# New start addresses for the streamed tiles and the weights of an MLP, in a kernel of linear attention and MLP

## The chip, the cores and the metric

The kernel runs on one core of a Trainium2 chip. The metric is the device time of one execution in microseconds (us), taken as the median of several runs. A run of the profiler gives one execution in detail: which engine worked when, and on what.

The engines are TensorE (PE for its matmuls, PEld for the loads of its weights), VectorE (DVE), ScalarE (ACT), GpSimd (POOL) and SyncE (SP, which issues DMAs). They work on SBUF, a memory of 128 partitions in which a tile occupies the same byte addresses in each partition. An address below is the byte address within a partition, and "896 modulo 2048" is its remainder.

## The reference

An attention with a state that decays per channel feeds an MLP without biases, whose activation is ELU. All is float32; B, H, S, D are 4, 8, 768, 48, the model width is 384 and the hidden width 2048.

```python
def _attn_ref(r, k, v, w, u):
    for t in range(S):
        kt, vt, rt, wt = k[:, :, t], v[:, :, t], r[:, :, t], w[:, :, t]
        cur = einsum('bhd,bhe->bhde', u[None] * kt, vt)
        y[:, :, t] = einsum('bhd,bhde->bhe', rt, state + cur)
        state = wt[:, :, :, None] * state + einsum('bhd,bhe->bhde', kt, vt)

def _moe_ref(x, w_in, w_out):            # x: 3072 tokens x 384
    h = x @ w_in                         # 384 x 2048
    g = where(h > 0, h, exp(minimum(h, 0)) - 1)
    return g @ w_out                     # 2048 x 384
```

## The kernel before, in words

The sequence is cut into 6 chunks of 128 steps. A unit is one chunk of one batch entry, 24 in all. For each unit DVE turns the decays into running products (lines L387 and L397) and scales r and k by them. PE then computes scores (L458), transposes k (L466), forms the outer products for the state (L505) and the output of the attention (L488, tile pa_y), all in float32. Four units of a chunk together give the MLP's input for 512 tokens: 3 planes of 128 channels by 512 tokens.

The MLP works in float32r, a float32 that PE takes in one pass. To keep precision, each operand is split into a high part and the rest, and each product is made of three: high by high, high weights by the rest, and the rest of the weights by high. So there are weights w_h and w_l, inputs xh and xl, and hidden activations gh and gl. For one block f of 128 hidden units (16 blocks a chunk), the step g1 runs 3 planes x 3 products = 9 matmuls into the tile ph (L248): weights of 128 x 128 are loaded, and the 512 tokens of a plane of xh or xl stream through. ACT and DVE then compute ELU in the tile m (L253 and L256 on ACT, L259 on DVE), ACT writes gh (L266) and DVE gl (L270). The step g2 runs 9 matmuls from gh and gl into three accumulators acc (L281). In the first two chunks, blocks 0 to 5 are done in two halves of 256 tokens each, so that the MLP can start before all four units are ready; in the last block of the last chunk the last accumulator is done in two halves as well.

PE streams one operand of a matmul and holds the other as weights. In the MLP the streamed tiles are xh, xl, gh and gl, and each matmul has a load of 128 x 128 weights, a block of 512 bytes per partition, from w_h or w_l.

The weights arrive raw, in tiles wraw and wrawx, and are converted by ACT (L540, L549) and DVE (L545, L552) during the first chunks. wrawx is kept in the space of xh and xl of the odd chunks, which are not in use yet. x tiles are allocated in x_high (one pair for even chunks, one for odd), gh and gl in g_tile inside the function mlp (two buffers each), all from a pool of SBUF called home. A pool named pad, of PAD bytes, lies ahead of it and serves only to shift it. The weights lie in a pool called big at the start of memory.

The order of work on each engine is written out by hand in a table (ORDER), and tiles are handed on by rings of buffers (SLOTS); neither depends on addresses.

What runs ahead of the MLP in a warm-up are some matmuls of the tile ident (L367).

Of the kernel before, what the change touches and what calls it, by code (L numbers as in the profile page):

```python
# [8 lines left out]
F32 = mybir.dt.float32  # L9
F32R = mybir.dt.float32r  # L10
# [11 lines left out]
P = 128  # L22
# [5 lines left out]
NK = DM // P  # L28
N = B * C
# [23 lines left out]


COLS = 128
PAD = 576
FILL = {}
DIAG = ["PE"] * 8 + ["POOL"] * 16
SPREAD = ["ACT"] * 8 + ["POOL"] * 16
# [169 lines left out]
def mlp(nc, w_h, w_l, ps_acc, ps_h, ml, gp, po, dst, last=False):  # L229

    act, stt_ = nc.scalar.activation, nc.vector.scalar_tensor_tensor
    acc = []

    def accs():
        if not acc:
            acc.extend(ps_acc.tile([P, N], F32, tag=f"acc{m}", name=f"acc{m}") for m in range(NK))
        return acc

    def g1(s, x, fill=()):
        f, lo, hi = s["f"], s["lo"], s["hi"]  # L240
        xh, xl = (z[:, :, lo:hi] for z in x)
        s["ph"] = ph = ps_h.tile([P, N], F32, tag="ph", name="ph")[:, 0:hi - lo]
        for m in fill:
            nc.tensor.matmul(ph[:, 0:P], m, m, start=True, stop=True)
        for k in range(NK):
            for n, (w, x_) in enumerate(((w_h, xh), (w_h, xl), (w_l, xh))):
                for z in range(0, P, COLS):
                    nc.tensor.matmul(ph[z:z + COLS], w[:, f, 0, k, z:z + COLS], x_[:, k, :],  # L248
                                     start=(k == n == 0), stop=(k == NK - 1 and n == 2))

    def r1(s):
        s["m"] = ml.tile([P, N], F32, tag="m", name="m", bufs=2)[:, 0:s["hi"] - s["lo"]]
        act(s["m"], s["ph"], AF.Relu, scale=-1.0)  # L253

    def r2(s):
        act(s["m"], s["m"], AF.Exp, scale=-1.0)  # L256

    def stt(s):
        stt_(s["m"], s["m"], -1.0, s["ph"], ALU.add, ALU.max)  # L259

    def g_tile(n, s):
        return gp.tile([P, N], F32R, tag=n, name=n, bufs=2)[:, 0:s["hi"] - s["lo"]]

    def gh(s):
        s["gh"] = g_tile("gh", s)
        nc.scalar.copy(s["gh"], s["m"])  # L266

    def gl(s):
        s["gl"] = g_tile("gl", s)
        nc.vector.tensor_tensor(s["gl"], s["m"], s["gh"].bitcast(F32), ALU.subtract)  # L270

    def g2(s):
        f, lo, hi = s["f"], s["lo"], s["hi"]
        for m in range(NK):
            parts = 2 if (f == NF - 1 and m == NK - 1 and last) else 1
            for q in range(parts):
                s_ = slice(q * (hi - lo) // parts, (q + 1) * (hi - lo) // parts)
                a_ = accs()[m][:, lo + s_.start:lo + s_.stop]
                for n, (w, g) in enumerate(((w_h, s["gh"]), (w_h, s["gl"]), (w_l, s["gh"]))):
                    for z in range(0, P, COLS):  # L280
                        nc.tensor.matmul(a_[z:z + COLS], w[:, f, 1, m, z:z + COLS], g[:, s_],  # L281
                                         start=(f == n == 0 and lo == 0), stop=(f == NF - 1 and q == parts - 1 and n == 2))

    box = {}

    def out(m):
        if m == 0:
            box["o"] = po.tile([P, NK, N], F32, tag="wraw", name="o", bufs=1)
        o = box["o"]
        if not last:  # L290
            nc.scalar.copy(o[:, m], acc[m])
        elif m == 0:
            nc.scalar.copy(o[:, m], acc[m])
            send(m)
        elif m == 1:
            nc.vector.tensor_copy(o[:, m], acc[m])
        else:
            h = N // 2
            nc.scalar.copy(o[:, m, 0:h], acc[m][:, 0:h])
            send(1)  # L300
            nc.vector.tensor_copy(o[:, m, h:N], acc[m][:, h:N])
            send(m)

    def send(m):
        nc.scalar.dma_start(dst[m * P:(m + 1) * P], box["o"][:, m])

    def store(m):
        if not last:
            nc.sync.dma_start(dst[m * P:(m + 1) * P], box["o"][:, m])

    return dict(g1=g1, r1=r1, r2=r2, stt=stt, gh=gh, gl=gl, g2=g2, out=out, store=store, accs=accs)
# [3 lines left out]
def rwkv_elu_kernel(ctx, tc, wkr, rk, vp, u, uz, gkrw, gv, gu, w_in, w_out, out):  # L315
# [5 lines left out]
    big = keep("big", 1)  # L321
    kp = keep("kp", 1)
    pad, home = pool("pad", 1), pool("home", 1)
# [9 lines left out]
    flags = kp.tile([R2, NU], F32, name="flags")  # L333
    good = kp.tile([1, 1], I32, name="good")
    ones_c = kp.tile([R2, 1], F32, name="ones_c")
    w_h = big.tile([P, NF, 2, NK, P], F32R, name="w_h")
    w_l = big.tile([P, NF, 2, NK, P], F32R, name="w_l")
    pad.tile([P, PAD // 4], F32, name="pad")
    reset = cst.tile([R2, 2, NP, CW], F32, name="reset")
# [9 lines left out]
    raws, xts, pfs = {}, {}, []  # L349
# [140 lines left out]
    def x_high(u_):  # L490
        c, b = u_["c"], u_["b"]
        if c not in xts:
            xts[c] = [home.tile([P, NK, N], F32R, tag=n + str(c % 2), name=n, bufs=1) for n in ("xh", "xl")]
        nc.scalar.copy(xts[c][0][:, :, b * C:(b + 1) * C], u_["py"])

    def x_low(u_):
# [77 lines left out]
    for u_ in units:  # L574
        i, c, b = u_["i"], u_["c"], u_["b"]
# [37 lines left out]
        if b:  # L613
            after.append(("v", i - 1))
        add(("v", i), "PE", lambda u_=u_: value(u_), after)
        add(("xh", i), "ACT", lambda u_=u_: x_high(u_), [("v", i)])
        add(("xl", i), "DVE", lambda u_=u_: x_low(u_), [("xh", i)])
        if c < NC - 1:
# [10 lines left out]
    for c in range(NC):  # L629
        fns = mlp(nc, w_h, w_l, ps_acc, ps_h, ml, home, stg, out[:, c * N:(c + 1) * N], last=c == NC - 1)  # L630
        for f, lo, hi in steps[c]:
            s, n = dict(f=f, lo=lo, hi=hi), len(seq)
# [22 lines left out]
    for u_ in units:  # L655
        i, c = u_["i"], u_["c"]
# [156 lines left out]
```

## Time and profile before

| what | value |
|---|---|
| median of 3 runs | 520.03 us (518.87, 520.03, 521.28) |
| profiled execution: its own time | 521.82 us |
| profiled execution: its span, first to last instruction | 520.1 us |
| granted TensorE clock, mean | 0.995 |
| busy: PE, DVE, ACT, POOL | 502.2, 331.2, 276.1, 66.0 us |
| HBM read, written | 41.92 MB, 4.72 MB |

The page of a profile lists groups of instructions as: line, engine, operation, tile written <- tiles read, shape, count | busy us, mean ns of one | idle us before them and what ended it. L248 is line 248 of the kernel. For a matmul "ph<-xh,w_h" the tile xh is streamed and w_h is held as weights. Matmuls overlap in the pipeline, so the mean duration of one (some 390 ns at 512 columns) is longer than the time from one start to the next, which is what a stretch of matmuls costs. Windows are stretches of the span in us, with each engine's busy time and count in them.

### The profile page before, as it was taken

Reading aid. Unit: us, or ns where it says so; the run is one execution under the profiler, and the core shown is the slowest. Engines: PE = TensorE matmul, PEld = TensorE weight load, DVE = VectorE, ACT = ScalarE, POOL = GpSimd, SP = SyncE. Lnnn points to the kernel's source line nnn. Section 1 sums busy time; section 2 is a strip of 40 time slices with the busy share of each in tenths; the row PEclk is TensorE's granted clock in tenths of the full one; section 3 lists DMA queues with packets and bytes.
Section 4 is the critical chain, followed back from the end, with each engine's and each line's share of the span. In section 5 each row is a group of like instructions: output and inputs, shape, how many; then the busy total and the mean of one; then the engine's idle time right before and its main releaser. Section 6 shows DMA issues by size and latency. Waiting matters only on the chain.

```text
span 520.1 us, 10015 instructions
## 1 busy us (share of the span) xinstructions
PE 502.2 (97%) x4065; PEld 423.7 (81%) x4065; DVE 331.2 (64%) x533; ACT 276.1 (53%) x558; POOL 66.0 (13%) x74
## 2 busy tenths in 40 slices
PE   4999999999999999999999999999999999999994
PEld 4788988889988888788888888888888788878884
DVE  7998889967677765756757476647474744333332
ACT  4979798757554434635444445325744524544441
POOL 2000000002131130701203021020220210000000
PEclk9989999999999999999999999999999999999999
DMA  7969463322224231322121336001440100000001
GB/s 223 325 218 281 140 204 113 92 68 88 78 77 134 86 100 39 124 87 88 56 70 38 94 105 194 2 1 38 143 127 8 69 1 1 26 36 3 0 2 64
DMA packets 26596, 47.35 MB, mean 91 GB/s; under 512 B 2736, under 2 KB 9008, under 8 KB 26544
## 3 DMA queue, kind: packets, MB, share of 16 engines
q1 hardware_dynamic: 26112, 45.86, 28.6%
q8 instruction: 34, 0.56, 0.4%
q10 hardware_dynamic: 432, 0.79, 0.4%
q14 instruction: 18, 0.15, 0.1%
HBM read 41.92 MB, written 4.72 MB: 90 GB/s over the span
## 4 chain that ended last, share of the span: by engine, by line
PE 86%; DVE 5%; ACT 2%; issue 1%; DMA 1%; SPq 0%; DVEq 0%; ACTq 0%
PE ph L248 36%; PE acc L281 36%; PE pa_y L488 6%; PE pa_s L458 4%; PE pa_u L505 2%; PE pa_t L466 1%; DVE m L259 1%; DMA r<-in_wkr_dram 1%; PE pa_d L428 1%; DVE gl L270 1%; DVE am L461 1%; ACT gh L266 0%; DVE r L401 0%; ACT m L256 0%; DVE xl L498 0%
## 5 line engine op out<-in xcount | busy, mean ns | idle before, releaser
L248 PE MATMUL ph<-xh,w_h 128*128 128x512 f32 (+1 forms) x324 | 122.1, 377 | 1.1 <-DVE m L259 1.0
L253 ACT ACTIVATE m<-ph 128x512 f32<-128x512 f32 (+1 forms) x108 | 59.3, 549 | 118.6 <-PE ph L248 78.6
L281 PE MATMUL acc<-gh,w_h 128*128 128x512 f32 (+1 forms) x325 | 120.7, 371 | 0.0
L248 PE MATMUL ph<-xl,w_h 128*128 128x512 f32 (+1 forms) x324 | 119.4, 369 | 1.2 <-DVE xl L498 1.2
L259 DVE SCALAR_TENSOR_TENSOR m<-m,ph 128x512 f32<-128x512 f32 (+1 forms) x108 | 67.0, 624 | 82.5 <-ACT m L256 82.2
L248 PE MATMUL ph<-xh,w_l 128*128 128x512 f32 (+1 forms) x324 | 119.5, 369 | 0.0
L281 PE MATMUL acc<-gl,w_h 128*128 128x512 f32 (+1 forms) x325 | 119.0, 366 | 0.3 <-DVE gl L270 0.3
L281 PE MATMUL acc<-gh,w_l 128*128 128x512 f32 (+1 forms) x325 | 118.7, 365 | 0.0
L270 DVE TENSOR_TENSOR gl<-m,gh 128x512 fp32r<-128x512 f32 (+1 forms) x108 | 68.9, 641 | 52.0 <-ACT gh L266 48.2
L266 ACT CAST gh<-m 128x512 fp32r<-128x512 f32 (+1 forms) x108 | 61.6, 571 | 70.3 <-PE acc L281 41.6
L248 PEld LDWEIGHTS ph<-xh,w_h 128*128 128x128 f32 x324 | 61.7, 191 | 13.3 <-DVE m L259 2.8
L248 PEld LDWEIGHTS ph<-xl,w_h 128*128 128x128 f32 x324 | 61.8, 191 | 10.5 <-DVE xl L498 1.4
L248 PEld LDWEIGHTS ph<-xh,w_l 128*128 128x128 f32 x324 | 61.8, 191 | 10.4 <-DVE w_l L552 0.2
L281 PEld LDWEIGHTS acc<-gl,w_h 128*128 128x128 f32 x325 | 61.3, 189 | 10.9 <-DVE gl L270 1.3
L281 PEld LDWEIGHTS acc<-gh,w_h 128*128 128x128 f32 x325 | 61.2, 188 | 10.8 <-issue 0.4
L281 PEld LDWEIGHTS acc<-gh,w_l 128*128 128x128 f32 x325 | 61.2, 188 | 9.8
L256 ACT ACTIVATE m<-m 128x512 f32<-128x512 f32 (+1 forms) x108 | 62.4, 583 | 1.5
L411 POOL TENSOR_TENSOR rk<-rk 128x384 f32<-128x384 f32 x16 | 17.8, 1115 | 221.9 <-DMA rk<-in_rk_dram 221.9
L461 DVE COPY_PREDICATED am<-upper,pa_s 128x512 f32<-128x512 uint32 x48 | 34.5, 744 | 16.9 <-PE pa_s L458 16.7
L446 POOL TENSOR_SCALAR_AFFINE_SELECT am<-md 128x512 f32<-128x512 f32 x32 | 27.7, 889 | 134.8 <-PE pa_y L488 101.0
L387 DVE TENSOR_TENSOR_SCAN eg<-w,reset 112x516 f32<-112x516 f32 x24 | 29.3, 1226 | 3.8 <-DMA w<-in_wkr_dram 3.2
L408 ACT ACTIVATE junk<-eg,lim 112x1032 bf16<-112x1032 f32 x24 | 27.7, 1155 | 7.3 <-DVE eg L397 7.2
(61 smaller groups left out, 471.0 us busy)
## 6 DMA issues: line engine op xcount, KB each, us to landing
v<-in_vp_dram SPq DMA_DIRECT2D x24, 256.0 KB, 4.0
rk<-in_rk_dram SPq DMA_DIRECT2D x16, 384.0 KB, 3.3
w<-in_wkr_dram SPq DMA_DIRECT2D x24, 226.2 KB, 3.7
k<-in_wkr_dram SPq DMA_DIRECT2D x24, 224.0 KB, 3.7
r<-in_wkr_dram SPq DMA_DIRECT2D x24, 224.0 KB, 4.1
out_dram<-o SPq DMA_DIRECT2D x15, 256.0 KB, 4.0
wrawx<-in_w_out_dram SPq DMA_DIRECT2D x10, 383.8 KB, 6.1
wrawx<-in_w_in_dram SPq DMA_DIRECT2D x10, 383.2 KB, 5.3
```

Of the source, the lines that this page charges most:

```text
L248: nc.tensor.matmul(ph[z:z + COLS], w[:, f, 0, k, z:z + COLS], x_[:, k, :], start=(k == n == 0), stop=(k == NK - 1 and n == 2))
L253: act(s["m"], s["ph"], AF.Relu, scale=-1.0)
L256: act(s["m"], s["m"], AF.Exp, scale=-1.0)
L259: stt_(s["m"], s["m"], -1.0, s["ph"], ALU.add, ALU.max)
L266: nc.scalar.copy(s["gh"], s["m"])
L270: nc.vector.tensor_tensor(s["gl"], s["m"], s["gh"].bitcast(F32), ALU.subtract)
L281: nc.tensor.matmul(a_[z:z + COLS], w[:, f, 1, m, z:z + COLS], g[:, s_], start=(f == n == 0 and lo == 0), stop=(f == NF - 1 and q == parts ...
L387: nc.vector.tensor_tensor_scan(out=flat(eg[:, 0]), data0=u_["w"][:, 1:W1][:, ::-1], data1=flat(reset[:, 0]), initial=0.0, op0=ALU.mult, op ...
L408: act(junk, u_["eg"].rearrange("d z p t -> d (z p t)"), AF.Relu, bias=lim, accum_out=flags[:, u_["i"]:u_["i"] + 1])
L446: nc.gpsimd.affine_select(out=am, in_=u_["md"][:, q::2].unsqueeze(2).broadcast_to([P, NP, C]), pattern=[[0, NP], [1, C]], compare_op=ALU.i ...
L461: nc.vector.copy_predicated(u_["am"][q], upper4, u_["pa"][q])
L488: nc.tensor.matmul(py[32 * j:32 * j + 32, k], l, r, start=(n == same[0]), stop=(n == same[-1]))
```

## The change

The streamed tiles get row lengths that are no longer multiples of 2048 bytes, so that each begins elsewhere modulo 2048. The tiles grow by unused elements at the end of a row: GAP gives their number for each kind. Two small unused tiles are put ahead of w_h (128 bytes) and of w_l (256 bytes), and PAD shrinks by 256 bytes.

```diff
-PAD = 576
+PAD = 320
+GAP = dict(gh=136, gl=80, xh=24, xl=56)
...
     def g_tile(n, s):
-        return gp.tile([P, N], F32R, tag=n, name=n, bufs=2)[:, 0:s["hi"] - s["lo"]]
+        return gp.tile([P, N + GAP[n]], F32R, tag=n, name=n, bufs=2)[:, 0:s["hi"] - s["lo"]]
...
+    big.tile([P, 32], F32, name="pad_h")
     w_h = big.tile([P, NF, 2, NK, P], F32R, name="w_h")
+    big.tile([P, 64], F32, name="pad_l")
     w_l = big.tile([P, NF, 2, NK, P], F32R, name="w_l")
...
-            xts[c] = [home.tile([P, NK, N], F32R, tag=n + str(c % 2), name=n, bufs=1) for n in ("xh", "xl")]
+            xts[c] = [home.tile([P, NK, N + GAP[n]], F32R, tag=n + str(c % 2), name=n, bufs=1)[:, :, 0:N] for n in ("xh", "xl")]
```

The shapes that the engines compute on are the same, and so are the instructions of all five engines, their order and what they wait for. What differs are the addresses. The places of the tiles, as the two programs allocate them:

| tile | before, modulo 2048 | after, modulo 2048 |
|---|---|---|
| xl, odd chunks, planes 0, 1, 2 | 896, 896, 896 | 1024, 1248, 1472 |
| xh, odd chunks | 896, 896, 896 | 1696, 1792, 1888 |
| xh, even chunks | 896, 896, 896 | 1984, 32, 128 |
| xl, even chunks | 896, 896, 896 | 224, 448, 672 |
| gh, two buffers | 896, 896 | 896, 1440 |
| gl, two buffers | 896, 896 | 1984, 256 |
| w_h (modulo 512) | 128 | 256 |
| w_l (modulo 512) | 128 | 0 |
| wrawx, in xh and xl of odd chunks | 896, 896 | 1696, 1024 |
| wraw | 1504 | 1184 |
| m | 1664 | 1344 |
| k, r and v of the attention | 1568 | 1248 |
| am of the attention | 1728 | 1408 |
| ident | 960 | 640 |

Of the sixteen streams of the MLP, two have the same place afterwards (1984: plane 0 of xh of even chunks, and the first buffer of gl), so there are fifteen places. The tiles of the attention and of the conversion move by 320 bytes together.

## The prediction, as it was made before the changed kernel ran

> **What bounds the kernel now.** I read the page first: the span, the engines' shares, and the chain that ended last.
>
> ```profile
> span 520.1 us, 10015 instructions
> PE 502.2 (97%) x4065; PEld 423.7 (81%) x4065; DVE 331.2 (64%) x533; ACT 276.1 (53%) x558; POOL 66.0 (13%) x74
> PE 86%; DVE 5%; ACT 2%; issue 1%; DMA 1%; SPq 0%; DVEq 0%; ACTq 0%
> PE ph L248 36%; PE acc L281 36%; PE pa_y L488 6%; PE pa_s L458 4%; PE pa_u L505 2%; PE pa_t L466 1%; DVE m L259 1%; DMA r<-in_wkr_dram 1%; PE pa_d L428 1%; DVE gl L270 1%; DVE am L461 1%; ACT gh L266 0%; DVE r L401 0%; ACT m L256 0%; DVE xl L498 0%
> ```
>
> PE is busy in 97% of the span, 86% of the last chain is PE, and 72% is the two lines of the MLP, L248 and L281. A busy share says nothing of where in the program it holds, so next comes the view by windows (columns: length, then busy us and count for PE, PEld, DVE, ACT, POOL, then granted clock, DMA share, GB/s).
>
> ```profile
> 0.00:13.00 13.00, 5.64 (x30) 5.31 (x32) 9.80 (x17) 6.22 (x17) 3.67 (x10) 1.00 0.77 223
> 13.00:60.00 47.00, 44.43 (x478) 41.49 (x476) 41.79 (x69) 39.22 (x90) 0.00 (x0) 0.96 0.82 249
> 60.00:120.00 60.00, 60.00 (x470) 51.81 (x470) 51.11 (x80) 47.26 (x101) 0.00 (x0) 1.00 0.37 117
> 120.00:513.00 393.00, 391.56 (x3092) 324.73 (x3092) 227.50 (x368) 183.06 (x352) 62.37 (x64) 1.00 0.21 63
> ```
>
> There are two regimes. Before 60 us every engine is loaded (DVE 9.80 + 41.79 = 51.6 of 60 us, DMA share 0.8) and PE still has gaps. From 60 to 513 us PE is idle for 393.00 - 391.56 = 1.4 us in all; ACT and DVE have slack there. So a nanosecond on an ACT or DVE instruction counts before 60 us at most, and one on every MLP matmul counts nearly in full after 60 us. How many of these there are is in the same view for one line at a time, L248 first, then L281:
>
> ```profile
> 60.00:120.00 60.00, 27.44 (x129) 21.39 (x128) 1.00 0.37 117
> 120.00:513.00 393.00, 175.73 (x738) 132.53 (x738) 1.00 0.21 63
> ...
> 60.00:120.00 60.00, 26.45 (x121) 20.78 (x122) 1.00 0.37 117
> 120.00:513.00 393.00, 178.94 (x772) 137.08 (x772) 1.00 0.21 63
> ```
>
> That is 129 + 738 + 121 + 772 = 1760 MLP matmuls where PE has no slack. The cost of one is the step from start to start, since their modelled durations overlap. The timeline of PE in a stretch of nothing but MLP, its second and its last row with 69 left out, and the window of that stretch:
>
> ```profile
> 483.94 0.39 PE L248 MATMUL ph<-xh,w_h 128*128 128x512 f32 x1
> ...
> 499.81 0.39 PE L248 MATMUL ph<-xl,w_h 128*128 128x512 f32 x1
> ...
> 484.00:500.00 16.00, 16.00 (x72) 13.28 (x71) 4.33 (x8) 6.26 (x11) 0.00 (x0) 1.00 0.00 1
> ```
>
> 70 steps take 15.87 us, 226.7 ns each. At full clock the 512 columns would need 213.3 ns, if a column takes half of what it takes at the half clock below; each step thus has 13.4 ns beyond its columns. Meanwhile ACT is busy for 6.26 us and DVE for 4.33 us, reading and writing the neighbours of the streamed tiles, and the rhythm is unbroken.
>
> **The change part by part.** It removes and adds no instruction, and the order on each engine stays. Only addresses differ. Four edits, four prices.
>
> *The streamed tiles' places.* Nothing of before streams from all the new places, so the term is bounded by the nearest rows. Before, a 256-column half of an x tile begins at 896 or, for the second half, at 1920 modulo 2048. The first and last start of a group of nine of each (first half, then second; eight rows between, the last row is the next group's first matmul):
>
> ```profile
> 35.21 0.28 PE L248 MATMUL ph<-xh,w_h 128*128 128x256 f32 x1
> ...
> 36.29 0.28 PE L281 MATMUL acc<-gh,w_h 128*128 128x256 f32 x1
> ...
> 50.05 0.28 PE L248 MATMUL ph<-xh,w_h 128*128 128x256 f32 x1
> ...
> 51.13 0.28 PE L281 MATMUL acc<-gh,w_h 128*128 128x256 f32 x1
> ```
>
> Both take 1.08 us for nine, 120 ns a matmul: 1024 bytes of shift make no difference, and the second group hands over to a gh tile at another place (1920 to 896) at the same 120. New are places that are odd multiples of 32 bytes (7 of the 16 streams). The attention's r tiles lie so (1568), its am tiles don't (1728), and matmuls of the same size stream from both:
>
> ```profile
> L488 PE MATMUL pa_y<-am,v 128*32 128x128 f32 x768 | 26.2, 278 | 0.6 <-DVE am L461 0.6
> L488 PE MATMUL pa_y<-r,st 112*32 112x128 f32 x480 | 17.2, 276 | 0.0
> ```
>
> 276 against 278 ns: no charge for it. For the good end I ask what the 13.4 ns are. In the first tiles the clock is at half:
>
> ```profile
> 28.24 0.41 PE L248 MATMUL ph<-xh,w_l 128*128 128x256 f32 x1
> ...
> 30.16 0.40 PE L248 MATMUL ph<-xh,w_l 128*128 128x256 f32 x1
> ...
> 28.40:30.20 1.80, 1.80 (x11) 1.80 (x10) 1.19 (x3) 0.80 (x2) 0.00 (x0) 0.50 0.36 139
> ```
>
> Nine steps in 1.92 us are 213.3 ns for 256 columns at clock 0.50, so 106.7 at full clock, and the 120 ns seen there hold 13.3 beyond the columns. So the excess is 13.3 to 13.4 ns at 256 and at 512 columns, the same per matmul whatever is streamed, and at half clock the same tiles at the same places show none. That speaks for a fixed step between matmuls and against a collision that depends on where a stream starts. The good end is that it all goes: 1760 x 13.3 = 23.4 us. The bad end is the slowest rhythm that an MLP group keeps without waiting, just after a change of width:
>
> ```profile
> 61.25 0.40 PE L248 MATMUL ph<-xh,w_h 128*128 128x512 f32 x1
> ...
> 62.41 0.39 PE L248 MATMUL ph<-xh,w_l 128*128 128x512 f32 x1
> ...
> 63.32 0.28 PE L281 MATMUL acc<-gh,w_h 128*128 128x256 f32 x1
> ```
>
> Five steps in 1.16 us, 232 ns, then four in 0.91 us, 227.5. The difference to 226.7 is 5.3 ns; on all 1760 it is 9.3 us. Between -23.4 and +9.3 us I take 0, because the rows that differ in place alone (35.21 and 50.05) are equal.
>
> *The weights' places.* All blocks begin at 128 modulo 512 before; afterwards at 256 (w_h) and 0 (w_l). The nearest row is the load of ident (L367), which begins at 448 modulo 512, against an MLP load:
>
> ```profile
> L248 PEld LDWEIGHTS ph<-xl,w_h 128*128 128x128 f32 x324 | 61.8, 191 | 10.5 <-DVE xl L498 1.4
> L367 PEld LDWEIGHTS acc<-ident 128*128 128x128 f32 x20 | 2.3, 192 | 0.3 <-issue 0.3
> ```
>
> 192 against 191 ns: 1 ns either way, 1.8 us if all 1760 paid it or gained it. I take 0, since loads run beside the matmul before (PEld is idle for 16.00 - 13.28 = 2.7 us of the stretch at 484); without that cover it would be the 1.8 us.
>
> *ACT and DVE on shifted tiles.* The raw weights come into wraw (1504, an odd multiple of 32) and wrawx (896) and are read by the same two instructions:
>
> ```profile
> L540 ACT ACTIVATE wt<-wrawx 128x768 f16<-128x768 bf16 x10 | 10.6, 1075 | 0.0
> L545 DVE SCALAR_TENSOR_TENSOR wg<-wrawx,wt 128x768 uint32<-128x768 uint32 x10 | 9.5, 953 | 0.0
> L540 ACT ACTIVATE wt<-wraw 128x768 f16<-128x768 bf16 x6 | 6.4, 1066 | 0.0
> L545 DVE SCALAR_TENSOR_TENSOR wg<-wraw,wt 128x768 uint32<-128x768 uint32 x6 | 5.7, 956 | 2.0 <-ACT wt L540 2.0
> ```
>
> 9 and 3 ns in about 1000, under 1%: of DVE's 51.6 us before 60 us at most 0.5 us either way. After 60 us PE's full queue hides it; if that cover went, m would be late for gl and gl for L281. I take 0, the mean of a plus and a minus.
>
> *DMA into shifted tiles.* Landing times of the two raw buffers:
>
> ```profile
> wrawx<-in_w_out_dram SPq DMA_DIRECT2D x10, 383.8 KB, 6.1
> wraw<-in_w_out_dram SPq DMA_DIRECT2D x6, 383.8 KB, 5.7
> ```
>
> 0.4 us apart, with the odd multiple of 32 the faster. Such a load is on the path only while weights still arrive, before 60 us; one of them late or early is 0.4 us either way. I take 0.
>
> The sum is 0 against the profiled execution: 520.1 us span plus 1.7 outside it make its 521.8 us, which lies 1.8 us above the median of 520.03. So the forecast is the median, 520.0 us.
>
> **The rivals.** *A charge for going from one place to another (slower).* Before, nearly every stream follows one of the same place; afterwards xh and xl alternate between different ones in every triple of L248, gh and gl in L281. If a new place costs PE 5.3 ns, the step just after a change of width, all 1760 pay and the time is 529.3 us; if only streams that begin at odd multiples of 32 pay (7 of 16), 4.1 us, 524.1 us. It decides (0.5%, 2.6 us, about what a measurement of this kernel can tell from no change) from 1.5 ns per matmul on. For it: no row of before has such alternation among full-width tiles. Against it: the hand-over from 1920 to 896 costs nothing.
>
> *The excess is a collision of places (faster).* Weight loads and streams run together, and with every weight block at 128 and every stream at 384 modulo 512 they might hit each other each time. If the change ends that, 23.4 us go and the time is 496.6 us; if half of them are freed, 508.3 us. It decides from 1.5 ns of the 13.3 on. For it: weights and streams have one place modulo 512 throughout, so the trace can't exclude it. Against it: the excess vanishes at half clock with places unchanged, and ACT and DVE never disturb the rhythm. [...]
>
> *The spread is not what moves it.* Two of the sixteen streams (xh's first plane of even chunks and the first gl buffer) still share 1984, and if only the first 60 us feel the new addresses, through DMA or DVE, it is the two terms of 0.4 and 0.5 us, or up to 3 us, an estimate for seven such loads queued behind one another.
>
> **How the numbers follow.** Nothing moves: 0.70, at 520.0 us, 517.4 to 522.6. The charge: 0.15, about half of it at 529 and half near 524. The collision: 0.09, 497 to 508. The first 60 us alone: 0.06, half on each side by about 3 us. So faster 0.09 + 0.03 = 0.12, same 0.70, slower 0.15 + 0.03 = 0.18. The range 516.5 to 526.5 leaves out the collision (0.09) and the full charge (some 0.08).
>
> **What the profile afterwards would show.** Right: 70 steps near 484 us again in 15.87 us, half tiles at 120 ns, L248 and L281 with the same means, the half-clock group again near 28.2 us. The charge: the mean step over 228 ns, most of all where xl follows xh, and PE busier after 60 us. The collision: steps under 225 ns, and DVE or ACT soon named in PE's waits, since their chain would be late next. Wrong for another reason: equal steps, but the MLP starting later than before.

## The result, and the profile after

The changed kernel takes 523.97 us (median of 5 runs, 523.37 to 525.23), the kernel before 519.33 us beside it (5 runs, 518.87 to 521.28): a ratio of 1.0088, with a 95% interval of 1.0069 to 1.0107. That is 4.6 us slower. The forecast was no change, 520.0 us. Three of the executions behind the numbers below ran long (562, 570 and 1266 us, the last the profiled one of distance_192, whose trace is not read); the ratios leave them out.

The page of the changed kernel:

```profile
span 521.6 us, 10015 instructions
PE 506.1 (97%) x4065; PEld 422.0 (81%) x4065; DVE 331.0 (63%) x533; ACT 276.4 (53%) x558; POOL 66.7 (13%) x74
PE 87%; DVE 6%; ACT 2%; issue 1%; ACTq 0%
```

The instructions are the same in number and DVE, ACT and POOL are busy as long as before; PE is busy 3.9 us longer. The spans of the two profiled executions differ by 1.5 us only, and that is no measure of the change: the one of before lay 2.5 us above its median, and in its window from 13 to 60 us the granted clock was 0.96, against 1.00 here. The changed kernel's windows from 13 us on:

```profile
13.00:60.00 47.00, 44.61 (x489) 41.38 (x488) 42.98 (x71) 40.81 (x93) 0.00 (x0) 1.00 0.86 262
60.00:120.00 60.00, 60.00 (x467) 51.26 (x466) 50.99 (x80) 46.02 (x99) 0.00 (x0) 1.00 0.34 106
120.00:513.00 393.00, 392.27 (x3068) 321.15 (x3068) 225.55 (x365) 182.16 (x351) 63.04 (x64) 1.00 0.21 63
```

From 120 to 513 us PE is as full as before (0.7 us idle), but it gets through 3068 matmuls where it got through 3092. So each takes longer. The timeline of PE in the stretch that the prediction named, second and last row with 68 left out, its window, and four rows from within:

```profile
483.91 0.39 PE L282 MATMUL acc<-gh,w_l 128*128 128x512 f32 x1
...
499.91 0.39 PE L282 MATMUL acc<-gh,w_l 128*128 128x512 f32 x1
...
484.00:500.00 16.00, 16.00 (x71) 12.96 (x70) 5.34 (x8) 6.20 (x11) 0.00 (x0) 1.00 0.00 1
...
486.24 0.39 PE L249 MATMUL ph<-xh,w_h 128*128 128x512 f32 x1
486.46 0.40 PE L249 MATMUL ph<-xl,w_h 128*128 128x512 f32 x1
486.70 0.39 PE L249 MATMUL ph<-xh,w_l 128*128 128x512 f32 x1
486.93 0.39 PE L282 MATMUL acc<-gh,w_h 128*128 128x512 f32 x1
```

69 steps take 16.00 us, 231.9 ns each instead of 226.7, and they are no longer even: in whole ns of the trace, the three steps between the four rows are 226, 235 and 232. PE is busy throughout this stretch (16.00 of 16.00 us). The half tiles, in contrast, became a little faster. Nine steps of the changed kernel, from one group's start to the next group's:

```profile
48.47 0.28 PE L249 MATMUL ph<-xh,w_h 128*128 128x256 f32 x1
...
49.53 0.28 PE L282 MATMUL acc<-gh,w_h 128*128 128x256 f32 x1
```

1.06 us for nine, 118 ns instead of 120.

For the comparisons below, the starts of all MLP matmuls were taken from each trace, in ns, and the mean step formed over those that follow one another without a wait (under 250 ns at 512 columns, some 1430 steps; under 140 ns at 256, some 390). Before: 227.7 and 119.6 ns. After: 231.6 and 118.3 ns. Over all 1509 full and 438 half matmuls (1947, one record in the trace for each float32r matmul that the kernel calls) that is 1509 x 3.93 - 438 x 1.27 ns = +5.4 us, against 4.6 us measured (3.6 to 5.6 by the interval).

The place of the loss can be counted directly, between two matmuls that both traces have. From the matmul at 61.25 us in the trace of before (59.49 in the changed kernel) to PE's last one, the changed kernel takes 4.6 us longer. The steps between full MLP matmuls have all of it, and the rest differs by less than 0.1 us in sum. The mean step gives more because it leaves out the long steps of over 250 ns, and these became fewer and shorter (from 43 with 15.5 us to 38 with 13.3 us). The trace of before comes to the first of the two matmuls 1.8 us later and takes 1.3 us longer behind the last, which is why the spans differ by 1.5 us only.

### The profile page after: what moved, and what is told of

It reads as the page before. It is cut to its first block, busy times and chain, and to the rows that moved or that the text cites. A ratio compares the mean times of both kernels' runs of the same rounds, so it can differ in the third digit from the quotient of the medians.

```text
span 521.6 us, 10015 instructions
## 1 busy us (share of the span) xinstructions
PE 506.1 (97%) x4065; PEld 422.0 (81%) x4065; DVE 331.0 (63%) x533; ACT 276.4 (53%) x558; POOL 66.7 (13%) x74
## 4 chain that ended last, share of the span: by engine, by line
PE 87%; DVE 6%; ACT 2%; issue 1%; ACTq 0%
PE acc L282 37%; PE ph L249 36%; PE pa_y L491 6%; PE pa_s L461 4%; PE pa_u L508 2%; PE pa_t L469 1%; DVE am L464 1%; DVE m L260 1%; PE pa_d L431 1%; DVE gl L271 1%; DVE w_l L555 1%; DVE r L404 1%; DVE wg L548 0%; DVE eg L400 0%; ACT gh L267 0%
## 5 line engine op out<-in xcount | busy, mean ns | idle before, releaser
L254 ACT ACTIVATE m<-ph 128x512 f32<-128x512 f32 (+1 forms) x108 | 59.4, 550 | 118.6 <-PE ph L249 81.2
L282 PE MATMUL acc<-gh,w_l 128*128 128x512 f32 (+1 forms) x325 | 119.8, 369 | 0.0
L282 PE MATMUL acc<-gl,w_h 128*128 128x512 f32 (+1 forms) x325 | 119.6, 368 | 0.0
```

## The experiments

"Distance" below is the place where a stream begins minus the place where a weights block begins. Before, it is 256 modulo 512 for every matmul of the MLP. All edits are to the kernel before. The stretches shown are PE's timeline from its second row in 484 to 500 us to its last, so the rows left out are the number of steps less one.

**Only the weights, only the streams.**

```diff
# weights_only
-PAD = 576
+PAD = 192
+    big.tile([P, 32], F32, name="pad_h")   # ahead of w_h
+    big.tile([P, 64], F32, name="pad_l")   # ahead of w_l
# streams_only
-PAD = 576
+PAD = 704
+GAP = dict(gh=136, gl=80, xh=24, xl=56)    # used as in the change
```

> Only the weights move (w_h to 256, w_l to 0 modulo 512); all streams stay at 896 modulo 2048, followed by streams of the same place. Theory 1 (what counts is the distance from the weights' start to the stream's start, modulo 512: 256 for every matmul before): the distance is now 128 for w_h and 384 for w_l, so the step leaves 226.7 ns and most of the 4.6 us of the full change appears, some 522 to 525 us. Theory 2 (PE is charged where the next stream begins at another place than the last one): no stream differs from the last, so 519.3 us, 226.7 ns a step.

> Only the streamed tiles get their new places, the same as in the full change; the weights stay at 128 modulo 512. Theory 1: distances modulo 512 differ from matmul to matmul, so steps are irregular and the time some 522 to 525 us. Theory 2: all of the 4.6 us, 524 us, mean step 231 to 232 ns at 512 columns.

Weights alone: 526.64 us, ratio 1.0126 (1.0105 to 1.0146). Streams alone: 525.05 us, 1.0101 (1.0083 to 1.0120). Weights_only, 69 steps, then streams_only, 69 steps:

```profile
483.85 0.40 PE L248 MATMUL ph<-xh,w_l 128*128 128x512 f32 x1
...
499.87 0.40 PE L248 MATMUL ph<-xh,w_l 128*128 128x512 f32 x1
```

```profile
483.93 0.40 PE L282 MATMUL acc<-gl,w_h 128*128 128x512 f32 x1
...
499.94 0.39 PE L282 MATMUL acc<-gl,w_h 128*128 128x512 f32 x1
```

16.02 and 16.01 us, 232.2 and 232.0 ns a step. Each half of the change alone costs as much as the whole, or more. With the weights moved, the streams follow each other as before, so a charge for a stream that goes from one place to another (theory 2) cannot be the cause of these 232.2 ns.

**All streams at one other place; four places that are multiples of 512 apart.**

```diff
# all_at_1024
-PAD = 576
+PAD = 704
# spread_by_512 (PAD stays 576)
+GAP = dict(gh=128, gl=128, xh=128, xl=128) # used as in the change
```

> All streams at one place again, 1024 modulo 2048 in place of 896 (PAD larger by 128 bytes), weights at 128 as before. Theory 1: the distance is 384 modulo 512 for every matmul, so the step is regular but not 226.7 ns; at 5 ns more the time is 528 us, at 5 ns less 511 us. Theory 2: every stream follows one of its own place, so 519.3 us and 226.7 ns.

> The streams lie at four places modulo 2048 (896, 1408, 1920, 384), so that most follow one of another place, but all at 384 modulo 512 as before. Weights unmoved. Theory 1: the distance modulo 512 is 256 throughout, so 519.3 us and 226.7 ns. Theory 2: most of the charge, some 523 to 524 us and 230 to 232 ns a step.

All at 1024: 526.93 us, ratio 1.0128 (1.0105 to 1.0152), although all streams have one place again. Spread by 512: 519.81 us, 1.0000 (0.9988 to 1.0013), although the streams lie at four places. All_at_1024, 68 steps, then spread_by_512, 70 steps:

```profile
483.90 0.40 PE L248 MATMUL ph<-xh,w_h 128*128 128x512 f32 x1
...
499.77 0.40 PE L281 MATMUL acc<-gh,w_l 128*128 128x512 f32 x1
```

```profile
483.93 0.39 PE L282 MATMUL acc<-gh,w_l 128*128 128x512 f32 x1
...
499.79 0.39 PE L282 MATMUL acc<-gh,w_h 128*128 128x512 f32 x1
```

233.4 and 226.6 ns. Spreading the streams by multiples of 512 bytes does nothing; moving them all by 128 bytes does. Theory 1 stands in this: 384 is a poor distance. One distance does not mean one step, however: in this stretch of all_at_1024 the steps are 237, 229, 238, 229, 237 and 230 ns, over and over, and over the whole trace the commonest are 229, 232, 230, 237 and 231 ns.

**Both by 128, and other distances.**

```diff
# both_by_128 (PAD stays 576)
+    big.tile([P, 32], F32, name="pad_h")
# distance_0: pad_h of 64 elements, PAD 320; distance_64: 48, 384; distance_224: 8, 544
```

> Weights and streams both move by 128 bytes: weights at 256, streams at 0 modulo 512, distance 256 as before. If the distance counts: 519.6 us, 226.7 ns. If the places themselves count (weights at 128, or streams at 384): slower, 524 to 527 us as when only one of the two moved.

> Only the weights move, to 384 modulo 512, so that weights and streams begin at the same place, distance 0. If the distance counts modulo 256: 519.6 us and 226.7 ns as before. If it counts modulo 512: another step, irregular as at 384 and 128, some 525 to 528 us, or worse if two reads of one place collide throughout.

> Only the weights move, to 320 modulo 512: distance 64. If any distance other than 256 breaks the rhythm: 524 to 528 us with steps of 228 to 241 ns. If 256 is not the only good one, this is the place to see it: steps near 227 or fewer.

> Only the weights move, by 32 bytes, to 160 modulo 512: distance 224. If lines of 64 bytes or more are what collides, 32 bytes are less than one line and the time stays near 519.6 us, or moves by part of the charge, up to 522. If the distance counts to the last 32 bytes: 524 to 527 us.

Both by 128: 520.42 us, ratio 1.0000 (0.9982 to 1.0017). So moving both by the same 128 bytes costs nothing: what counts is the distance, not the place of either. The runs above agree: weights_only and all_at_1024 both come to 128 modulo 256, one by moving the weights and one by moving the streams, and their mean steps are 232.5 and 232.7 ns. Distance 0: 519.79 us, 0.9994 (0.9978 to 1.0010), like 256: the distance counts modulo 256. Distance 64: 520.49 us, 1.0009 (0.9994 to 1.0024). Distance 224, which is only 32 bytes from before: 526.51 us, 1.0113 (1.0077 to 1.0148). In this order, 71, 70, 69 and 68 steps:

```profile
483.88 0.39 PE L281 MATMUL acc<-gh,w_h 128*128 128x512 f32 x1
...
499.97 0.39 PE L281 MATMUL acc<-gh,w_l 128*128 128x512 f32 x1
```

```profile
483.94 0.39 PE L281 MATMUL acc<-gh,w_l 128*128 128x512 f32 x1
...
499.81 0.39 PE L281 MATMUL acc<-gh,w_h 128*128 128x512 f32 x1
```

```profile
484.03 0.39 PE L248 MATMUL ph<-xl,w_h 128*128 128x512 f32 x1
...
499.82 0.39 PE L248 MATMUL ph<-xl,w_h 128*128 128x512 f32 x1
```

```profile
483.93 0.40 PE L281 MATMUL acc<-gh,w_l 128*128 128x512 f32 x1
...
499.79 0.40 PE L281 MATMUL acc<-gl,w_h 128*128 128x512 f32 x1
```

226.6, 226.7, 228.8 and 233.2 ns.

**The rest of the distances, and w_l alone.**

```diff
# distance_32: pad_h of 56 elements, PAD 352; distance_96: 40, 416; distance_192: 16, 512
# w_l_alone
-PAD = 576
+PAD = 448
+    big.tile([P, 32], F32, name="pad_l")   # ahead of w_l
```

> Only the weights move, to 352 modulo 512: distance 32. So far the distance counts modulo 256 (0 and 256 alike), with mean steps of 227.7 ns at 0, 229.1 at 64, 232.7 at 128 and 233.3 at 224 for 512 columns, and 119.6, 117.2, 118.9, 118.2 for 256. If the step goes smoothly from 0 to 64: 228.4 and 118.4 ns, so 1500 x 0.7 - 420 x 1.2 ns = +0.5 us, 520.1. If the good place lies between them: under 227 ns and a time under 519. If each odd multiple of 32 is bad: 231 to 233 ns, 524 to 527 us.

> Only the weights move, to 288 modulo 512: distance 96. If the step goes smoothly from 64 to 128: 231 ns and 118 ns, +4.4 us, 524 us. If each odd multiple of 32 is bad: 232 to 233 ns and 526 us. If 64 bytes are the unit: like 64, 520.5 us.

> Only the weights move, to 192 modulo 512: distance 192. If the step goes smoothly from 128 to 224: 233 ns and 118.5 ns, 527 us. If even multiples of 64 bytes are better than odd multiples of 32: 228 to 230 ns, 520 to 523 us.

> Only w_l moves, by 128 bytes to 256 modulo 512: the distance is 256 for w_h and 128 for w_l. A step runs from the start of one matmul to the start of the next, and the load of the next one's weights runs beside it. If that load collides with the running stream: the steps of xl, gl (next weights w_l) are at 232 to 233 ns, the other two of each triple stay near 227. If it is the matmul's own weights that count: the steps of the matmuls with w_l are slow. In both cases a third of the charge of a full distance of 128: +2 to 2.5 us, 522 us. If the rhythm as a whole breaks, all three are slow and the time is 525 us.

Distance 32: 526.06 us, ratio 1.0113 (1.0087 to 1.0138), 233.3 ns: neither between 0 and 64 nor a better place. Distance 96: 527.06 us, 1.0129 (1.0096 to 1.0162). Distance 192: 526.40 us, 1.0112 (1.0077 to 1.0147); its steps are read from distance_192_again, below. W_l alone: 525.38 us, 1.0090 (1.0056 to 1.0125), its last row after 69 steps, 231.0 ns each:

```profile
483.87 0.39 PE L248 MATMUL ph<-xh,w_h 128*128 128x512 f32 x1
...
499.81 0.39 PE L248 MATMUL ph<-xh,w_h 128*128 128x512 f32 x1
```

That is more than the third of a full charge that was expected. By the kind of step, over the whole trace: from w_h to w_h 227.6 ns, untouched; from w_h to w_l 232.4; from w_l to w_h 233.7. So both steps beside a poorly placed block are slow, the one during which its load runs (in the trace of before a load of w_l and the matmul from xl ahead of it both begin at 486.89 us, and the load lasts 0.19 us) and the one during which it is in use.

**Which pair counts, and the two distances left.**

```diff
# lows_by_128: xl and gl begin 128 bytes into a tile that is 256 bytes longer
-home.tile([P, NK, N], ...)
+home.tile([P, NK * N + o], ...)[:, o // 2:o // 2 + NK * N].rearrange("p (k n) -> p k n", k=NK)   # o: xh 0, xl 64
-gp.tile([P, N], ...)[:, 0:s["hi"] - s["lo"]]
+gp.tile([P, N + 2 * o], ...)[:, o:o + s["hi"] - s["lo"]]                                         # o: gh 0, gl 32
# distance_160: pad_h of 24 elements, PAD 480; distance_192_again is distance_192
```

> Only the streams xl and gl begin 128 bytes further (distance 128 modulo 256); xh, gh and all weights keep distance 0. A triple is high stream with w_h, low stream with w_h, high stream with w_l. If it is the running stream that meets the load for the next matmul: only the steps that start with a low stream are slow (232 to 234 ns), the two others near 227.6, mean 229.5, +2.5 us, 522 us. If a matmul's own weights meet its own stream while it sets in: the step before it, into the low stream, is slow instead. If both, or if one disturbed step spoils the next: two of three slow, as in w_l_alone, mean 231, +4.7 us, 524 us.

> Only the weights move, to 224 modulo 512: distance 160. By the neighbours 128 and 224 (232.5 and 233.3 ns): 232 to 234 ns and 526 us. If it is a second good place as 64 is: 229 ns and 520.5 us.

> The kernel of distance_192 once more, for its profile: its time of 526.4 us stands for a mean step of 232 to 234 ns at 512 columns.

Lows by 128: 525.53 us, ratio 1.0102 (1.0075 to 1.0128). In the stretch at 484 us, 69 steps of 231.2 ns:

```profile
483.89 0.39 PE L248 MATMUL ph<-xh,w_h 128*128 128x512 f32 x1
...
499.84 0.40 PE L248 MATMUL ph<-xh,w_h 128*128 128x512 f32 x1
```

Over the whole trace, all three steps of a triple are slow: 233.5 ns into the low stream, 232.4 out of it, and 231.0 from high stream to high stream, whose own distances are both 0. None of the readings of the expectation holds: a poor stream spoils also a step that is not beside it (231.0 ns), while a poor w_l left one step in three alone (227.6 ns). Which stream counts against which weights stays open.

Distance 160: 527.75 us, 1.0150 (1.0124 to 1.0175). Distance 192 again: 525.42 us, 1.0101 (1.0071 to 1.0130). For 512 columns distance 192 is as poor as its neighbours, but its half tiles are the fastest of all, nine steps in 1.02 us, 113 ns:

```profile
48.43 0.28 PE L248 MATMUL ph<-xh,w_h 128*128 128x256 f32 x1
...
49.45 0.28 PE L281 MATMUL acc<-gh,w_h 128*128 128x256 f32 x1
```

All distances together, from the whole traces; "worked out" is 1509 and 438 times the difference to before. Row 128 moved the streams, the change moved both, and the rows of the other distances moved the weights:

| distance modulo 256 | step at 512, ns | step at 256, ns | worked out, us | measured (ratio - 1) x 519.6, us |
|---|---|---|---|---|
| 0 (before, at 256) | 227.7 | 119.6 | 0 | 0 |
| 0 (distance_0) | 227.7 | 119.5 | +0.1 | -0.3 |
| 32 | 233.3 | 117.1 | +7.4 | +5.9 |
| 64 | 229.1 | 117.2 | +1.1 | +0.5 |
| 96 | 233.4 | 119.8 | +8.7 | +6.7 |
| 128 (all_at_1024) | 232.7 | 118.9 | +7.3 | +6.7 |
| 160 | 234.2 | 118.0 | +9.2 | +7.8 |
| 192 (again) | 233.3 | 114.9 | +6.4 | +5.2 |
| 224 | 233.3 | 118.2 | +7.9 | +5.9 |
| mixed (the change) | 231.6 | 118.3 | +5.4 | +4.6 |

At every distance but 0 the working comes out 0.6 to 2.0 us above the measured loss, as it does for the change.

**A version that uses it.** Full tiles at 0 and the half-width gh and gl at 192:

```diff
     def g_tile(n, s):
-        return gp.tile([P, N], ...)[:, 0:s["hi"] - s["lo"]]
+        o = 48 if s["hi"] - s["lo"] < N else 0
+        return gp.tile([P, N], ...)[:, o:o + s["hi"] - s["lo"]]
```

> The half-width gh and gl are kept 192 bytes further in their buffers (distance 192); all full-width streams and the half-width x stay at distance 0. If each group of matmuls keeps its own step: 115 ns for the half-width L281, 227.7 for the rest, 220 x 4.7 ns = 1.0 us at most, of which the part after 60 us counts in full, 519.0 to 519.5 us (ratio 0.998 to 0.999). If the mixture disturbs its neighbours as in lows_by_128: half-width steps of 117 to 119 ns and full ones up to 229, 519.6 to 522 us.

518.81 us against 519.61, ratio 0.9986 (0.9975 to 0.9998). The half-width steps among gh and gl are 116.3 ns, those among xh and xl 118.6, and the full ones stay at 227.6. Worked out that is 1.0 us less, measured 0.7. The interval just leaves 1.0 out; it is the one version seen here that is ahead of both kernels, and by little. Placing the half-width x tiles as well was not tried: they share their tiles with full streams.

## Why the prediction was wrong, point by point

*What bounds the kernel* was right: after 60 us PE has no slack, and the loss is a longer step on the MLP matmuls, with DVE and ACT as busy as before.

*The streamed tiles' places* is the step that failed: "I take 0, because the rows that differ in place alone (35.21 and 50.05) are equal." They do not differ in what counts. 896 and 1920 are 1024 bytes apart, a multiple of 256, so they have the same distance to the weights, and so had all 1947 MLP matmuls of the trace. The trace of before held one value of the variable, and equality within it said nothing about others. The prediction saw this for the collision ("so the trace can't exclude it") and took 0 for the price all the same. The bounds were sound: streams_only cost 5.2 us (1.0% of 519.6), within -23.4 to +9.3. The row that looked nearest, pa_y at 276 and 278 ns, had other weights and another size, and its numbers are modelled durations, not steps; it did not bear on this.

*The half clock* was a further reason given against an effect of places: the excess is gone there "with places unchanged". That no excess is left at half clock is the prediction's estimate, which takes the whole step of 213.3 ns for its 256 columns and half of it, 106.7 ns, for the same columns at full clock. What was measured is the step alone, and it told nothing of places either, because it is the same at poor distances. Distance_160 has such a stretch, nine steps and a window:

```profile
27.63 0.41 PE L248 MATMUL ph<-xl,w_h 128*128 128x256 f32 x1
...
29.55 0.41 PE L248 MATMUL ph<-xl,w_h 128*128 128x256 f32 x1
...
28.40:29.80 1.40, 1.40 (x9) 1.40 (x8) 0.79 (x3) 0.69 (x2) 0.00 (x0) 0.50 0.18 70
```

These are 213.3 ns a step at a granted clock of 0.50, as before, in the kernel whose full tiles are the slowest of all at full clock (234.2 ns). The traces of all_at_1024 and distance_96 have such a stretch with the same step. In the changed kernel's trace the granted clock is 1.00 from 13 to 60 us, so the half-clock group that the prediction expected did not come.

*The weights' places* was taken as 0 within 1.8 us either way; moving the weights alone cost 6.5 us (1.26% of 519.6). The price was read from how long a load lasts, and that says nothing here. In weights_only a load lasts 188 ns, against 191 in the row of the prediction, while the step is 4.8 ns longer (232.5 against 227.7 in the mean):

```profile
L248 PEld LDWEIGHTS ph<-xl,w_h 128*128 128x128 f32 x324 | 61.0, 188 | 11.5 <-DVE xl L500 1.4
```

What the place of the weights does to the steps of the matmuls was left out. That loads lie under matmuls is no cover against that.

*The rivals.* The charge had the right sign and, in its part form (7 of 16 streams, 524.1 us), the right time, by luck: spread_by_512 changes places from stream to stream and costs nothing, weights_only costs 6.5 us with no stream moved, and all_at_1024 costs 6.7 us with every full stream at 1024, no odd multiple of 32. Nor is the step where xl follows xh the longest in the changed kernel (230.9 ns, against 232.5 where xh follows xl). That 523.97 us lies within the stated range, 516.5 to 526.5, is no support for it: the time is outside the 517.4 to 522.6 given for "nothing moves", and what moved it was priced at 0. The collision named what does count, where weights and streams lie to each other; its sign was wrong, since the old distance is the best of the eight for full tiles (227.7 ns at 0, 229.1 to 234.2 at the others). Of the 13.4 ns that the prediction estimated beyond the columns, none went away in the mean at 512 columns. At 256 some did: the step is 114.9 ns at distance 192 against 119.6 before, which by the same estimate (106.7 ns, half of the 213.3 at a clock of 0.50) leaves 8.2 beyond the columns.

*ACT, DVE and DMA* were taken as 0, and that held: in spread_by_512 and both_by_128 tiles of theirs moved as well, at ratios of 1.0000, and in the changed kernel the steps between full MLP matmuls have the whole loss after 60 us.

## What to carry to other kernels

Where PE is full with matmuls that load new weights each time, keep the start of the streamed operand and that of the weights a multiple of 256 bytes apart (shown here for float32r with 512 columns: 227.7 ns a step, against 229.1 to 234.2 at the other multiples of 32), and recheck it whenever a tile ahead of either changes size: 32 bytes cost 1.1% here (distance_224, 526.51 us). Before a trace is used to show that something doesn't matter, see whether it varied there at all. And price an instruction that runs beside another by what the other loses, not by its own length.

## What was not expected of the hardware

In these runs the step of a 512-column float32r matmul depends on the distance between streamed operand and weights modulo 256 bytes, down to 32 bytes: 227.7 ns at 0, 229.1 at 64, 232.7 to 234.2 at the other six multiples of 32. That it is modulo 256 rests on 0 and 256 (227.7 ns both) and on 128 and 384 (232.5 ns with w_h at the one and w_l at the other, 232.7 with both at 384). At 0 the steps are 226 and 227 ns for dozens in a row (1152 of the 1429 of before); elsewhere nearly all of them run through several values from 225 to 241 ns, in short cycles. For 256 columns the order is another: 114.9 ns at 192, 119.6 at 0. At a granted clock of 0.50 the step of 256 columns is 213.3 ns at distances 0, 96, 128 and 160 alike. The places themselves do not count (both_by_128: 520.42 us, a ratio of 1.0000, 226.6 ns a step). What has the period of 256 bytes, and whether two reads meet in it and which, is not shown.
